# Products of the first four units written to idle tiles, and the second and third input sets loaded earlier

## The chip, the cores and the metric

The kernel runs on one core of a Trainium2 chip. The metric is the time of one execution on the device in microseconds; the median of several runs is given. Where the text speaks of a profiled execution, it is one execution that the hardware profiler recorded.

## The reference

```python
def _attn_ref(r, k, v, w, a, b):            # all (4, 8, 768, 40)
    state = zeros(B, H, D, D)
    for t in range(S):
        y[:, :, t] = einsum('bhd,bhde->bhe', r[t], state)
        Sa = einsum('bhde,bhe->bhd', state, a[t])
        state = state * w[t][..., None, :] - einsum('bhd,bhe->bhde', Sa, b[t])
        state = state + einsum('bhd,bhe->bhde', v[t], k[t])

def reference(**kwargs):
    x = _attn_ref(...)                       # -> (4, 768, 320)
    u = x + ((x^T @ U) @ V)^T
    x = u + relu(u @ w_ch1) @ w_ch2
    return four softmax-attention experts on x, top 2 of 4 by a gate, mixed
```

Only the first stage, the recurrence, is touched. All of it is float32.

## The kernel before

The recurrence is computed in chunks of 64 steps. There are 12 chunks and two pairs of batches, so 24 units; a unit is eight pairs of heads wide. Instead of stepping through time, a unit forms 64x64 products of its inputs (TensorE), inverts triangular blocks (VectorE) and passes a state to the next chunk.

The inputs w, a, b, k come packed in 16 sets (ld) of 128 rows, 1028.5 KB each. A set m has rows 0:40 and 64:104 for a unit of its own, and in the rows between a half of a third unit, a guest: sets 0 and 1 hold units 0 and 1 and the halves of unit 2, sets 2 and 3 units 3, 4 and the halves of 5. `slot(j)` (L95) gives set j its place: sets 0 and 1 two tiles ldt, sets 2 and 3 a part of the tiles xs that is written much later, sets 4 and 5 ldt again.

The steps around the change, each a generator whose next part one letter of a hand-written string ORDER_R (L44) runs:

- m, `loads` (L177): DMAs of the sets on SP's queue. Set 0 is loaded before the string begins (L464 to 467) and so is the first part of set 1; sets 1 to 3 come in three parts, the later ones whole.
- d, `scaled(j)` (L183), all on VectorE: a scan of w into P (L195), a reciprocal and a reverse scan (L200, L203), the scaled b and k into bkt (L208), the scaled a (F, L216), and two DMAs of F into the unit's tile ga (L219).
- g, `sent(j)` (L166): DMAs of the guest's rows from P, bkt and F to the guest's tiles P_g, bkt_g and ga (L164). P and bkt have two buffers each, P_g and bkt_g one.
- f, `front(u)` (L223), in five parts: transposes of P (pt) with their eviction (L233, L235); transposes of bkt in two halves (pb, L243, L244); the products of bkt and ga in two halves (pg, L255), which ACT evicts over bkt itself (L258). After the second half POOL copies four 32x256 blocks into lx (L263), masks two blocks into ga (L266) and copies two into m21 (L270).
- l, `more`/`tick`: one VectorE step of `lanes(g)` (L275), which inverts the 32x32 blocks of four units together. It starts with a transpose of lx (L279), so it needs the lx copies of all four units of its group.
- z, `ready` (L445), POOL memsets of uv, xu, sbd with st, and rbd; y, `firsts` (L451), the first loads of v (uv) and r (rbd, uvt, rpt).

Every engine runs its instructions in the order in which the string brings them (manual_schedule, L471); only semaphores make one engine wait for another. SP's queue issues all of the DMAs here and waits in order too. `later`/`passed` (L141, L154) put off some VectorE work by a count of steps of the string; a step added to the string lowers these counts as well.

In the string the products of units 0, 1, 2 and 3 end at positions 38, 51, 65 and 90; the memsets of sbd and st come at 88, the one of rbd at 105, the first loads into rbd and uvt at 106.

Of the kernel before, what the change touches and what calls it, by code (L numbers as in the profile page):

```python
# [11 lines left out]
F32 = mybir.dt.float32  # L12
# [3 lines left out]
AF = mybir.ActivationFunctionType  # L16
# [25 lines left out]

WAIT = (2, 3, 3)
ORDER_R = (  # L44
    'zddlllllldllllmgdlmgdlzfdldlglfmfgfzdgfdmfllyfgmlfffmfdfdfmmddllfflglmlgdffddgdglgllffldzl',
    'ffglldllllmlllfzylflllldflllflylfffldllflgldflflglffldlggylllfllgdmBffllAfflflflfffgAldlll',
    'BlmdlllfdfBgABAfqBAllfqlqBAddlgllldgmpdpldBlgllAqpgllfBAlffBAqfqqfpBAppflgllldddllffBmlffl',
    'qplfllqfqldpdlglflAlqffflBAgqplBdAgBlAfpqBpAplmlldldlfgdllgpqqBllllAflfglplAlBpfplAlBllAfl',
    'llfqBpfAmBqgqpdAlflldqlldlllllflffplqqgBlddfflllpplglfmlAdBggfdqllfpBABAflpllqBllplqlfddll',
    'glflqlfdfplBlfflmdpgqABfpfqlqldfABpABpplAllgfAqgBldqmAlfpdfdlplglffgBgllfplfddlfqllpffAfdl',  # L50
    'lgfqlqlAfllflllmlllBlAfABppABpgqfBqlqAddppfgllAllBlqdqllpdfggBlqlqldffAlBgAlBfpAqlpqBlffll',
    'ffflfllpflflfllpulpqAlBplAqlqBAllulqBllAlpqBpAxBlqlllxlllAlppqllxxlBAlllqulpBAqlqlBlABplpl',
    'AllppBxqllllqlllllAqlllpBplqqlABullplqBAllBAlpqplquBAllpqlpxxllluBApqpBlAqqlBAlluBAlqqppAq',
    'qpxlllullxxqppqllpqulplqlBplllxxllx',
)


def recurrence(ctx, tc, ld, vin, rv, ident, xs, keep, wpool, mix):
# [40 lines left out]
    BK, GA, PC, LX, M21, TF, UP = {}, {}, {}, {}, {}, {}, {}

    def load_ld(j, a=0, b=LDW):
        nc.sync.dma_start(slot(j)[:, a:b], ld[j, :, a:b])
# [63 lines left out]
    def sent(j):  # L166

        m, r = divmod(j, 2)
        f3 = slot(j)[:, :3 * PP * C].rearrange("p (k q t) -> p k q t", k=3, t=C)
        away(guests[0], PF[3 * m + r], r)  # L170
        yield
        away(guests[1], BKT[3 * m + r], r)
        yield
        away(GA[3 * m + 2][:, r], f3[:, 2], r)
        yield

    def loads():  # L177
        for j in range(1, NSET):
            for y in parts[j == 1:] if j < 4 else ((0, LDW),):
                load_ld(j, *y)  # L180
                yield

    def scaled(j):  # L183

# [38 lines left out]
    def front(u):  # L223

        g, uu = divmod(u, GU)
        c, bp = divmod(u, NBP)
        P, early = PF[u], u < GU
        pc = PC[u] = const.tile([128, PP], F32, tag="pc", bufs=16, name=f"pc{u}")
        nc.scalar.activation(pc, P[:, :, C], AF.Copy)
        pt = ps.tile([128, 4, 2, D], F32, tag="f", bufs=3, name=f"pt{u}")  # L230
        for p in range(4):
            for b in range(2):
                nc.tensor.matmul(pt[64 * b:64 * b + 64, p], P[:, 2 * p + b, :C],  # L233
                                 ident.rearrange("p (r e) -> p r e", r=2)[:, :, :D], start=True, stop=True)
# [815 lines left out]
```

## Time and profile before

| | us |
|---|---|
| median of 3 runs (lowest, highest) | 854.38 (853.5, 856.28) |
| the profiled execution, whole | 858.54 |
| its span, first to last instruction | 856.8 |

| engine | busy in the span, us | share |
|---|---|---|
| PE (TensorE) | 780.3 | 91% |
| PE's weight loads | 666.2 | 78% |
| DVE (VectorE) | 579.5 | 68% |
| ACT (ScalarE) | 469.9 | 55% |
| POOL (GpSimd) | 323.9 | 38% |

The recurrence takes about the first 325 us. There DVE is busy in nearly every slice of the page but the first two, and PE works at a share that rises from 0.5 to nearly 1; after that PE alone is nearly always busy.

How to read it: times are microseconds from the start of the span, unless marked ns. L258 is line 258 of the kernel. In a timeline a row has start, duration, engine, line, operation, tile written <- tile read, the shape and the count of what was merged; in brackets the idle time of that engine before it and what ended that. In a list of waits a row has who waited for whom, the sum in us, the number of times and the longest. SPq is the queue of SyncE, whose durations are those of issuing a DMA, not of the transfer. PEclk is the granted TensorE clock, 1.00 for 2.4 GHz and 0.50 for 1.2 GHz.

### The profile page before, as it was taken

Reading aid. Unit: us, or ns where it says so; the run is one execution under the profiler, and the core shown is the slowest. Engines: PE = TensorE matmul, PEld = TensorE weight load, DVE = VectorE, ACT = ScalarE, POOL = GpSimd, SP = SyncE. Lnnn points to the kernel's source line nnn. Section 1 sums busy time; section 2 is a strip of 40 time slices with the busy share of each in tenths; the row PEclk is TensorE's granted clock in tenths of the full one; section 3 lists DMA queues with packets and bytes.
Section 4 is the critical chain, followed back from the end, with each engine's and each line's share of the span. In section 5 each row is a group of like instructions: output and inputs, shape, how many; then the busy total and the mean of one; then the engine's idle time right before and its main releaser. Section 6 shows DMA issues by size and latency. Waiting matters only on the chain.

```text
span 856.8 us, 22703 instructions
## 1 busy us (share of the span) xinstructions
PE 780.3 (91%) x9100; PEld 666.2 (78%) x9100; DVE 579.5 (68%) x1388; ACT 469.9 (55%) x1125; POOL 323.9 (38%) x456
## 2 busy tenths in 40 slices
PE   5666989989999897989899999999999999999997
PEld 4555888988898687877678888887778788887875
DVE  6599999988998997448624131322268868778773
ACT  3534867766677678723323231312168757767672
POOL 5664464536545324315513220202027344244430
PEclk9787999998999999899999999999999999999999
DMA  5554256555545364512100100000000010000101
GB/s 166 171 143 158 78 171 164 151 144 150 137 144 145 87 171 114 130 54 83 47 1 25 34 2 1 1 1 0 1 1 2 1 47 2 16 32 2 47 2 47
DMA packets 53201, 61.47 MB, mean 72 GB/s; under 512 B 31208, under 2 KB 38376, under 8 KB 51560
## 3 DMA queue, kind: packets, MB, share of 16 engines
q1 hardware_dynamic: 53096, 60.02, 24.6%
q8 instruction: 72, 1.18, 0.6%
q14 instruction: 33, 0.27, 0.1%
HBM read 47.46 MB, written 4.13 MB: 60 GB/s over the span
## 4 chain that ended last, share of the span: by engine, by line
PE 54%; DVE 19%; DMA 6%; issue 5%; ACT 4%; POOL 2%; SPq 1%; DVEq 0%; POOLq 0%; ACTq 0%
PE po L943 4%; PE ph L743 3%; PE pa L760 3%; PE ph L740 3%; PE pa L761 3%; PE pa L762 3%; PE ph L741 3%; PE ph L739 3%; PE tp L930 3%; DVE lt L288 3%; DVE tmp L285 3%; PE pn L403 2%; PE pw L343 2%; PE ps L890 2%; PE ps L889 2%
## 5 line engine op out<-in xcount | busy, mean ns | idle before, releaser
L913 POOL TENSOR_TENSOR P<-P,sm 128x128 f32<-128x128 f32 (+2 forms) x92 | 82.9, 931 | 127.6 <-DVE sm L903 115.4
L747 DVE SCALAR_TENSOR_TENSOR hl<-ph,hh 128x512 fp32r<-128x512 f32 x60 | 41.1, 690 | 118.6 <-ACT hh L746 116.1
L746 ACT ACTIVATE hh<-ph 128x512 fp32r<-128x512 f32 x60 | 35.1, 594 | 108.5 <-PE pa L762 101.2
L894 ACT ACTIVATE P<-ps,mx 128x640 f32<-128x640 f32 (+4 forms) x96 | 60.5, 634 | 26.1 <-DVE mx L892 18.1
L285 DVE TENSOR_TENSOR tmp<-lt 128x30 f32<-128x30 f32 (+9 forms) x180 | 70.3, 390 | 3.9
L288 DVE TENSOR_TENSOR lt<-lt,tmp 128x30 f32<-128x30 f32 (+9 forms) x180 | 69.0, 384 | 3.7
L892 DVE CUSTOM_DVE_ANT_0 ps<-ps,neg 128x640 f32<-128x640 f32 (+4 forms) x96 | 59.0, 639 | 7.6 <-PE ps L890 6.5
L263 POOL COPY lx<-bkt 32x256 f32<-32x256 f32 x64 | 30.0, 469 | 87.9 <-ACT bkt L258 85.8
L403 PE MATMUL pn<-rbd,uvt 128*128 128x128 f32 x384 | 54.9, 293 | 7.3 <-DMA uvt<-in_rin 5.7
L776 POOL TENSOR_TENSOR t<-t,ul 128x512 f32<-128x512 f32 x12 | 15.4, 1294 | 116.8 <-DVE t L775 116.7
L255 PE MATMUL pg<-ga,bkt 128*128 128x128 f32 x256 | 40.1, 318 | 19.6 <-DMA ga<-ldt 14.3
L403 PEld LDWEIGHTS pn<-rbd,uvt 128*128 128x128 f32 x384 | 49.6, 204 | 9.5 <-issue 4.9
L930 PE MATMUL tp<-ident,P 128*128 128x128 f32 x336 | 52.0, 276 | 1.8 <-ACT pt L934 0.8
L255 PEld LDWEIGHTS pg<-ga,bkt 128*128 128x128 f32 x256 | 36.6, 226 | 21.6 <-issue 12.7
L346 ACT ACTIVATE uv<-pw 32x320 f32<-32x320 f32 x96 | 41.1, 428 | 18.4 <-PE pw L343 16.7
L739 PE MATMUL ph<-uh,w 128*128 128x512 f32 x120 | 47.1, 399 | 1.7 <-ACT uh L728 1.6
L740 PE MATMUL ph<-ul,w 128*128 128x512 f32 x120 | 47.7, 397 | 0.6 <-DVE ul L729 0.6
L741 PE MATMUL ph<-uh,w 128*128 128x512 f32 x120 | 47.3, 396 | 0.0
L761 PE MATMUL pa<-hl,w 128*128 128x512 f32 x120 | 47.1, 392 | 0.0
L930 PEld LDWEIGHTS tp<-ident,P 128*128 128x128 f32 x336 | 39.4, 140 | 9.2 <-POOL P L913 2.7
L943 PE MATMUL po<-pt,vals 128*64 128x256 f32 (+3 forms) x320 | 45.1, 397 | 1.4 <-DVE o L959 1.0
L762 PE MATMUL pa<-hh,w 128*128 128x512 f32 x120 | 46.2, 391 | 0.0
(217 smaller groups left out, 2239.8 us busy)
## 6 DMA issues: line engine op xcount, KB each, us to landing
ldt<-in_ld SPq DMA_DIRECT2D x12, 1028.5 KB
uvt<-in_rin SPq DMA_DIRECT2D x48, 128.0 KB
rpt<-in_rin SPq DMA_DIRECT2D x24, 256.0 KB
rbd<-in_rin SPq DMA_DIRECT2D x48, 96.0 KB
uv<-in_vin SPq DMA_DIRECT2D x48, 80.0 KB
out<-o SPq DMA_DIRECT2D x24, 160.0 KB
ga<-ldt SPq DMA_DIRECT2D x28, 80.0 KB
room<-in_w SPq DMA_DIRECT2D x7, 320.0 KB
```

The source lines that it names most:

```text
L255: nc.tensor.matmul(pg[:, p], bkt[:, h * HP + p].rearrange("p k t -> p (k t)"), ga[:, :, h * HP + p], start=True, stop=True)
L285: nc.vector.tensor_tensor(tv, L[:, s + 1:, s:s + 1].to_broadcast([128, n, s]), L[:, s:s + 1, :s].to_broadcast([128, n, s]), op=OP.mult)
L288: nc.vector.tensor_tensor(L[:, s + 1:, :s], L[:, s + 1:, :s], tv, op=OP.add)
L403: nc.tensor.matmul(pn[h][:, p], ut[:, h * HP + p].rearrange("p r t -> p (r t)"), rbd[u % 2][:, :, h * HP + p], start=True, stop=True)
L739: nc.tensor.matmul(ph, w[:, 0, f], uh[:, ft], start=ft == 0, stop=False)
L740: nc.tensor.matmul(ph, w[:, 0, f], ul[:, ft], start=False, stop=False)
L741: nc.tensor.matmul(ph, w[:, 1, f], uh[:, ft], start=False, stop=False)
L761: nc.tensor.matmul(pa[ft], w[:, o:o + m], hl, start=False, stop=False)
L762: nc.tensor.matmul(pa[ft], w[:, 2 * DM - FT[2][0] + o:2 * DM - FT[2][0] + o + m], hh, start=False, stop=last)
L913: nc.gpsimd.tensor_tensor(p, p, sm[:, i:i + 1].to_broadcast([128, w]), op=OP.mult)
L930: nc.tensor.transpose(pt[:, j - j0], P[:, c:c + 128], ident)
L943: nc.tensor.matmul(po[64 * r:64 * r + 64, s0:w], VS[b][:, j, HD * e:HD * e + HD], PT[r][:, j, s0:], start=j == 0, stop=j == i1 - 1, skip_g ...
```

## The change

Three edits, all in `recurrence`.

1. The products of units 0 to 3 (`early`) are evicted not over bkt but to four tiles that are idle at that time, viewed in bkt's shape: rbd0, rbd1, uvt0 and uvt1 (`rooms`). POOL reads them from there (gm).
2. POOL's two masks into ga and two copies into m21 become a generator of their own, `kept(u)`, with a letter k. In the string each k stands right behind the f that ends its unit's products. Beside k's that are added and m's that are taken out, the order of all other steps is the same, also with the works that are put off.
3. Sets 0 and 1 are loaded on SP ahead of the string, in three parts each. Set 2 is loaded in two parts on ACT's queue at the string's start. Sets 3 and later are loaded whole, set 3 by the first m left in the string; it stands behind unit 1's products and ahead of the DMAs of F for unit 3.

```diff
-    def load_ld(j, a=0, b=LDW):
-        nc.sync.dma_start(slot(j)[:, a:b], ld[j, :, a:b])
+    rooms = [t.rearrange("p r q t -> p (r q t)").rearrange("p (q r t) -> p q r t", q=PP, r=2) for t in rbd] + uvt
+    def load_ld(j, a=0, b=LDW, queue=nc.sync):
+        queue.dma_start(slot(j)[:, a:b], ld[j, :, a:b])
...
     def loads():
-        for j in range(1, NSET):
-            for y in parts[j == 1:] if j < 4 else ((0, LDW),):
-                load_ld(j, *y)
-                yield
+        for j in range(3, NSET):
+            load_ld(j)
+            yield
...
-            nc.scalar.activation(bkt[:, hs], pg, AF.Copy)
+            gm = GM[u] = rooms[u] if early else bkt
+            nc.scalar.activation(gm[:, hs], pg, AF.Copy)
...
-                        nc.gpsimd.tensor_copy(LX[g][q, uu * PP:uu * PP + PP], bkt[q, :, r, 32 * i:32 * i + 32])
-                for r in range(2):
-                    ... affine_select(ga[z, r], bkt[z, :, r], ...)
-                for r in range(2):
-                    ... tensor_copy(m21[q], bkt[q, :, r, 32:])
+                        nc.gpsimd.tensor_copy(LX[g][q, uu * PP:uu * PP + PP], gm[q, :, r, 32 * i:32 * i + 32])
...
+    def kept(u):
+        ga, gm = GA[u], GM[u]
+        m21 = M21[u] = const.tile([128, PP, 32], F32, tag="m21", bufs=AHEAD + 1, name=f"m21{u}")
+        for r in range(2):
+            ... affine_select(ga[z, r], gm[z, :, r], ...)
+        for r in range(2):
+            ... tensor_copy(m21[q], gm[q, :, r, 32:])
+        yield
...
-    for a, b in parts:
-        load_ld(0, a, b)
-    load_ld(1, *parts[0])
+    for j in range(2):
+        for a, b in parts:
+            load_ld(j, a, b)
...
+    for a, b in (parts[0], (0, n)):
+        load_ld(2, a, b, nc.scalar)
...
+            "k": chain(*[kept(u) for u in range(NU)]), ...
```

The first two lines of the string, before and after:

```diff
-    'zddlllllldllllmgdlmgdlzfdldlglfmfgfzdgfdmfllyfgmlfffmfdfdfmmddllfflglmlgdffddgdglgllffldzl',
-    'ffglldllllmlllfzylflllldflllflylfffldllflgldflflglffldlggylllfllgdmBffllAfflflflfffgAldlll',
+    'zddlllllldllllgdlgdlzfdldlglffgfzdgfkdfllyfglfffkmfdfdfddllffklglmlgdffddgdglgllffldzlfkfg',
+    'lldllllmlllfzylflllldflllfklylfffldllflgldfklflglffldlggylllfllgdmBfkfllAfflflfklfffgAldll',
```

## Rows read from the trace of the kernel before

**Rows 1.** Busy time by stretch, 42 to 100 us.

```profile
core 0: us, PE busy (x) PEld busy (x) DVE busy (x) ACT busy (x) POOL busy (x), PEclk, DMA share, GB/s
...
42.00:60.00 18.00, 13.04 (x140) 11.73 (x141) 17.02 (x35) 6.45 (x15) 11.45 (x22) 0.84 0.58 151
60.00:80.00 20.00, 9.74 (x155) 8.84 (x152) 18.62 (x46) 7.04 (x18) 8.88 (x15) 0.74 0.55 174
80.00:100.00 20.00, 18.04 (x465) 16.24 (x464) 19.48 (x41) 16.51 (x38) 10.29 (x16) 1.00 0.18 49
```

**Rows 2.** Timeline of DVE, 0 to 45 us.

```profile
13.79 0.69 DVE L216 SCALAR_TENSOR_TENSOR ldt<-ldt,P 128x512 f32<-128x512 f32 x1 [0.79 <-DMA ldt<-in_ld]
...
17.24 1.31 DVE L195 TENSOR_TENSOR_SCAN P<-x,hot 128x520 f32<-128x520 f32 x1 [2.73 <-PE pt L233]
...
18.82 1.45 DVE L203 TENSOR_TENSOR_SCAN x<-x,hot 128x520 f32<-128x520 f32 x1
24.31 1.45 DVE L208 TENSOR_TENSOR bkt<-x 128x1024 f32<-128x1024 f32 x1 [4.04 <-DMA x<-in_ld]
...
30.84 1.32 DVE L208 TENSOR_TENSOR bkt<-x 128x1024 f32<-128x1024 f32 x1 [0.20 <-ACT pc L229]
32.08 0.88 DVE L216 SCALAR_TENSOR_TENSOR x<-x,P 128x512 f32<-128x512 f32 x1
...
36.05 1.24 DVE L195 TENSOR_TENSOR_SCAN P<-ldt,hot 128x520 f32<-128x520 f32 x1 [3.07 <-DMA ldt<-in_ld]
...
41.57 1.97 DVE L279 STREAM_TRANSPOSE lt<-lx 128x1024 f32<-128x1024 f32 x1 [2.76 <-POOL lx L263]
```

**Rows 3.** Timeline of POOL, 0 to 50 us.

```profile
16.64 2.55 POOL L263 COPY lx<-bkt 32x256 f32<-32x256 f32 x4 [9.17 <-ACT bkt L258]
19.26 2.17 POOL L266 TENSOR_SCALAR_AFFINE_SELECT ga<-bkt 64x512 f32<-64x512 f32 x2
...
24.03 2.24 POOL L266 TENSOR_SCALAR_AFFINE_SELECT ga<-bkt 64x512 f32<-64x512 f32 x2
...
30.69 2.97 POOL L263 COPY lx<-bkt_g 32x256 f32<-32x256 f32 x4 [3.62 <-ACT bkt_g L258]
33.73 1.35 POOL L266 TENSOR_SCALAR_AFFINE_SELECT ga<-bkt_g 64x512 f32<-64x512 f32 x2
35.04 0.84 POOL L270 COPY m<-bkt_g 32x256 f32<-32x256 f32 x2
35.93 1.20 POOL L448 MEMSET sbd<- 128x640 f32 x2
37.08 0.66 POOL L448 MEMSET st<- 128x320 f32 x2
39.84 1.69 POOL L263 COPY lx<-bkt 32x256 f32<-32x256 f32 x4 [2.11 <-ACT bkt L258]
```

**Rows 4.** Timeline of ACT, 0 to 45 us.

```profile
23.39 1.99 ACT L129 ACTIVATE ga<-zero 128x1024 f32<-128x1024 f32 x2
...
38.70 1.09 ACT L258 ACTIVATE bkt<-pg 128x512 f32<-128x512 f32 x2 [5.31 <-DMA bkt_g<-bkt]
```

**Rows 5.** Waits of SP's queue, 0 to 60 us: sum, times, longest.

```profile
SPq L164 <- POOL m L270: 4.4, 1, 4.4
```

**Rows 6.** Timeline of SP's queue, 0 to 50 us.

```profile
0.82 2.28 SPq L102 DMA_DIRECT2D ldt<-in_ld  x5
...
16.05 1.51 SPq L219 DMA_DIRECT2D ga<-ldt  x2
...
30.80 0.58 SPq L102 DMA_DIRECT2D ldt<-in_ld  x1
```

**Rows 7.** DMA rate in 40 equal slices of 0 to 60 us.

```profile
GB/s 0 106 374 359 407 40 20 105 257 66 201 87 120 137 323 134 294 191 332 100 89 121 406 187 68 96 93 72 104 77 99 335 386 231 144 107 112 56 115 55
DMA packets 5190, 9.90 MB, mean 165 GB/s; under 512 B 1912, under 2 KB 2168, under 8 KB 4928
```

**Rows 8.** Timeline of PE, 0 to 45 us.

```profile
12.16 3.78 PE L255 MATMUL pg<-ga,bkt 128*128 128x128 f32 x16 [1.81 <-DMA ga<-ldt]
...
19.27 2.02 PE L255 MATMUL pg<-ga,bkt 128*128 128x128 f32 x16 [1.05 <-DMA ga<-ldt]
...
26.74 3.25 PE L255 MATMUL pg<-ga,bkt_g 128*128 128x128 f32 x16 [3.72 <-DMA ga<-ldt]
```

More of the change, by code (lines that the diff above doesn't have):

```diff
@@ L44 @@
 ORDER_R = (
-    'zddlllllldllllmgdlmgdlzfdldlglfmfgfzdgfdmfllyfgmlfffmfdfdfmmddllfflglmlgdffddgdglgllffldzl',
-    'ffglldllllmlllfzylflllldflllflylfffldllflgldflflglffldlggylllfllgdmBffllAfflflflfffgAldlll',
[L47 to L54, printed above, removed]
+    'zddlllllldllllgdlgdlzfdldlglffgfzdgfkdfllyfglfffkmfdfdfddllffklglmlgdffddgdglgllffldzlfkfg',
+    'lldllllmlllfzylflllldflllfklylfffldllflgldfklflglffldlggylllfllgdmBfkfllAfflflfklfffgAldll',
+    'lBlmdlllfdfkBgABAfqBAllfqlqBAddlgllldgmpdpldBlgllAqpgllfBAlffkBAqfqqfpBAppflgllldddllffkBm',
+    'lfflqplfllqfqldpdlglfklAlqffflBAgqplBdAgBlAfpqBpAplmlldldlfkgdllgpqqBllllAflfglplAlBpfplAl',
+    'BllAflllfkqBpfAmBqgqpdAlflldqlldlllllflffkplqqgBlddfflllpplglfmlAdBggfdqllfkpBABAflpllqBll',
+    'plqlfddllglflqlfdfkplBlfflmdpgqABfpfqlqldfkABpABpplAllgfAqgBldqmAlfpdfdlplglffkgBgllfplfdd',
+    'lfqllpffkAfdllgfqlqlAfllflllmlllBlAfkABppABpgqfBqlqAddppfgllAllBlqdqllpdfggBlqlqldffkAlBgA',
+    'lBfpAqlpqBlffllffkflfllpflflfkllpulpqAlBplAqlqBAllulqBllAlpqBpAxBlqlllxlllAlppqllxxlBAlllq',
+    'ulpBAqlqlBlABplplAllppBxqllllqlllllAqlllpBplqqlABullplqBAllBAlpqplquBAllpqlpxxllluBApqpBlA',
+    'qqlBAlluBAlqqppAqqpxlllullxxqppqllpqulplqlBplllxxllx',
 )
@@ L98, in recurrence @@
     mix.spare = lambda: fpool.tile([128, 2 * (S // 4)], F32, tag="lx", name="spare")
[L99 to L102 removed]
+    BK, GA, GM, PC, LX, M21, TF, UP = {}, {}, {}, {}, {}, {}, {}, {}
+    def load_ld(j, a=0, b=LDW, queue=nc.sync):
+        queue.dma_start(slot(j)[:, a:b], ld[j, :, a:b])
     def load_v(u):
@@ L248, in front @@
         ga = GA[u]
-        m21 = M21[u] = const.tile([128, PP, 32], F32, tag="m21", bufs=AHEAD + 1, name=f"m21{u}")
         if uu == 0:
@@ L262, in front @@
                         q = slice(64 * r + 32 * i, 64 * r + 32 * i + 32)
-                        nc.gpsimd.tensor_copy(LX[g][q, uu * PP:uu * PP + PP], bkt[q, :, r, 32 * i:32 * i + 32])
-                for r in range(2):
-                    z = slice(64 - 64 * r, 128 - 64 * r)
-                    nc.gpsimd.affine_select(ga[z, r], bkt[z, :, r], [[0, PP], [1, C]], OP.is_gt, 0.0, base=0,
-                                            channel_multiplier=-1)
-                for r in range(2):
-                    q = slice(64 * r, 64 * r + 32)
-                    nc.gpsimd.tensor_copy(m21[q], bkt[q, :, r, 32:])
+                        nc.gpsimd.tensor_copy(LX[g][q, uu * PP:uu * PP + PP], gm[q, :, r, 32 * i:32 * i + 32])
             if h and uu == GU - 1:
@@ L273, in front @@
             yield
+    def kept(u):
+        ga, gm = GA[u], GM[u]
+        m21 = M21[u] = const.tile([128, PP, 32], F32, tag="m21", bufs=AHEAD + 1, name=f"m21{u}")
+        for r in range(2):
+            z = slice(64 - 64 * r, 128 - 64 * r)
+            nc.gpsimd.affine_select(ga[z, r], gm[z, :, r], [[0, PP], [1, C]], OP.is_gt, 0.0, base=0,
+                                    channel_multiplier=-1)
+        for r in range(2):
+            q = slice(64 * r, 64 * r + 32)
+            nc.gpsimd.tensor_copy(m21[q], gm[q, :, r, 32:])
+        yield
     def lanes(g):
@@ L475, in recurrence @@
             "d": chain(*[scaled(j) for j in range(NSET)]),
-            "g": chain(*[sent(j) for j in range(NSET)]), "m": loads(), "y": firsts(), "f": fronts(), "z": ready(), "l": more(),
+            "g": chain(*[sent(j) for j in range(NSET)]), "m": loads(), "y": firsts(), "f": fronts(),
+            "k": chain(*[kept(u) for u in range(NU)]), "z": ready(), "l": more(),
             "u": mix.weights(mix.sources()[0], ldt, (guests[0].rearrange("p q t -> p (q t)"), hot)),
```

## The prediction

> **What bounds the kernel now.** I read the views in this order: busy time by stretch, then the timeline of each engine in the first 45 us with what ended its pauses, then the DMA's rate there. Busy time by stretch [rows 1] shows VectorE (DVE) as the engine without slack from 42 us on: 17.0 of 18 us, 18.6 of 20, 19.5 of 20, while TensorE (PE) is at 13.0 and 9.7 of the first two stretches. Its pauses there add up to 2.9 us between 122 instructions, so none is a wait worth the name. The last one that is ends at 41.57 us: 2.76 us, for POOL's copies into lx (L263), and with it the first group's `lanes` starts, by its transpose (L279) [rows 2]. So everything after 41.57 us runs on one engine's clock, started by the fourth unit's lx copies. A change ahead of that point is worth what it moves 41.57 to, and no more.
>
> What made the copies late: POOL began them at 39.84, after an eviction (L258) that ACT started at 38.70 after 5.31 us of waiting for the DMA bkt_g<-bkt [rows 3, 4]. The eviction overwrites bkt in place, so it must wait until unit 5's guest rows have been sent out of it. That DMA in turn stood on SP for 4.4 us behind POOL's m21 copies (L270) [rows 5], which still read bkt_g of unit 2. This circle is what the change opens.
>
> **The change part by part.** Times are the profiled execution's: span 856.8 us, whole time 858.54, that is 4.16 above the median 854.38. I work out a difference and take it off the median.
>
> *Evictions to idle tiles* (units 0 to 3, eight ACTIVATEs): same count, same 128x512 shape (1.09 us for two [rows 4]), no new instruction. Removed: the wait for bkt_g<-bkt ahead of those of units 0, 1 and 3, and the hold that POOL's readers had on bkt and bkt_g. The rooms are rbd and uvt; rbd's memset and the first loads into both stand behind `kept(3)` in program order anyway, so nothing new waits for them.
>
> *`kept` as a step of its own*: each k stands right behind the fifth f of its unit, so POOL's order is what it was: lx, affine selects (L266), m21, unit by unit, then sbd and st, then unit 3's lx. Taking loads and k's out, the whole later order is unchanged, also the delayed DVE works. Cost and gain 0.
>
> *Loads*: SP issued five ahead in 2.28 us [rows 6], so a sixth costs 0.46 us in time in which SP is idle. Two for set 2 go to ACT, which has nothing else to do until DVE's first scan has made P; at about 0.6 us each (one load's issue is 0.58 [rows 6]) I cost them at nothing, and at 1.2 us on ACT if that cover were gone. They put 3.09 MB up front instead of 1.8 MB. The slices of 1.5 us in 3 to 7.5 us moved 374, 359 and 407 GB/s [rows 7]; begun at some 2.6 us, three sets and P_g are through by 2.6 + 3.17 MB / 385 GB/s = 10.8 us, ahead of unit 0's ga rows, which land at 12.16, where PE's first product starts [rows 8]. So I leave unit 0's products and the first lx copies at 16.64 where they are [rows 3], and keep a delay of up to 1.5 us for the range.
>
> Gone from SP are the loads that stood between the guests' DMAs. Unit 1's ga rows (16.05 us, 1.51 of issue, product at 19.27, so landed 1.7 us after issue [rows 6, 8]) go out at 14.7 and land at 17.9; the product takes 2.0 us and the eviction is done by 20.8. Unit 2's ga rows are issued by 20.25 and land at 22.0 instead of 26.74, where PE had waited 3.72 us for them [rows 8]; the eviction, behind ACT's two blank tiles (1.99 us [rows 4]), is done at 25.6. Set 3, now whole, is issued at 20.3 to 20.9. Set 4 took from 31.38 to 36.05, 4.7 us, to land [rows 2, 6], so set 3 lands at 25.6. Unit 3's ga rows wait on SP for their blank tile (23.5) and are there by 26.8, its product is evicted by 29.9. Set 4 goes out at 26.4 to 27.0 and lands at 31.7.
>
> DVE then runs set 2's steps in 13.8 to 18.6 (set 1's F no longer waits 0.79 us for its load [rows 2], and set 2 is there), set 3's from 25.6, set 4's two scans from 31.7, and is free for `lanes` at 34.4. If nothing else were late, `lanes` would start there, 7.1 us earlier.
>
> *What is late next: POOL.* From 16.64 on it never waits, as each eviction (20.8, 25.6, 29.9) is there before it comes to it. Its bare sum up to unit 3's lx, by rows without a long DVE operation beside them [rows 3]: lx 1.69, affine selects 1.35, m21 0.84, thrice: 11.64; sbd and st 1.20 + 0.66 = 1.86; the last lx 1.69; with 0.3 for the gaps 15.5. That ends at 32.1 us.
>
> But POOL and DVE hold each other up. With a scan at 17.24 beside it lx took 2.55 (0.86 over), the selects with a scan at 18.82 took 2.17 (0.82 over), with the product into bkt at 24.31 2.24 (0.89 over), and lx with two such operations, at 30.84 and 32.08, took 2.97 (1.28 over) [rows 2, 3]. Five DVE operations cost POOL 3.85 us, 0.77 each. The memsets beside the scan at 36.05 took nothing more. Before, sets 3 and 4 mostly met an idle POOL or its memsets; now POOL has no pause, so eight such operations fall on its copies and selects: set 2's bkt and F, set 3's two scans, bkt and F, set 4's two scans. 8 x 0.77 = 6.2 us, and lx ends at 38.3. The bounds: no hold at all, then DVE's 34.4 decides; each of the eight for its whole length (six of 1.24, two of 0.69 [rows 2], 8.8 us), 40.9. I take 0.77 since it comes from the same tiles and engines.
>
> The Trainium skill (SBUF — State Buffer, on the ports that DVE and GpSimd share) says that the pair is an exclusive lock, and that a DVE operation with two SBUF inputs and a GpSimd one that reads SBUF fully block each other. By that rule the whole lengths would count, and `lanes` would start at 40.9 us, 0.7 us earlier than now; the measured 0.77 is less, and the sum goes by it.
>
> So `lanes` starts at 38.3 us instead of 41.57: 3.2 us earlier. From there to 100 us DVE has no pause to lose it in [rows 1], the later order is the old one, and set 5 and unit 4's ga rows, which follow on SP, come some 6 us earlier, so they don't take over. Forecast: 854.38 - 3.2 = 851.2, with 34.4 to 40.9 as the far ends of `lanes`, 847.2 to 853.7.
>
> **The rivals.**
> (1) *The hold is cheap.* Sets 3 and 4 meet POOL's memsets or its waits, and POOL ends at 33 to 36: 5.5 to 7.1 us earlier, at 6.4 us 848.0. For it: the memsets are free, and a later set 4 would meet them. Against it: four of four rows in which POOL and a long DVE operation overlap show the price.
> (2) *Nothing left.* Each of the eight operations holds POOL for its whole length (40.9), or 1 to 2 us of delay at unit 0's ga rows on top of the forecast, leaves 0 to 1.5 us: 853.6. For it: each eats most of 3.2 us. Against: the measured price and the rate in the first slices.
> (3) *The preloads crowd out unit 0, and it gets slower.* Set 1 is now ahead of unit 0's ga rows on SP's queue and set 2 beside it on ACT's. PE's first product waits for them. At the page's rate of the mixed stretches, say 165 GB/s (the mean of 0 to 60 us [rows 7]), 3.17 MB last until 21.8 us, the rows land 11 us later, and since set 2's operations are then past when POOL begins, `lanes` starts at 28 + 15.5 + 4.6 = 48: 6.6 us later, 861. It decides from about 250 GB/s down: there the rows land 4.8 us later, which takes back the 3.2 us and the 1.5 us of set 2's holds that fall away. Against: 359 to 407 GB/s in just this traffic.
>
> **How the numbers follow.** Forecast (2 to 4.4 us earlier, 850.0 to 852.4) 0.58; rival 1 0.18; rival 2 0.18; rival 3 0.06. A measurement of this kernel tells about 0.3%, 2.6 us, from no change, so faster means below 851.8: rival 1 and about 0.65 of the forecast, 0.18 + 0.38 = 0.56. Slower is rival 3, 0.05 of it beyond 0.3%. The same is the rest, 0.39. The range must leave out at most 0.2: from 847.8 (rival 1's most likely half is in) to 853.8 (most of rival 2 is in).
>
> **What would show it.** In the trace after: no wait of ACT's first eight L258 for bkt_g<-bkt; POOL's idle time between 16.6 us and unit 3's lx near 0, and lx and selects of units 2 and 3 longer than 1.69 and 1.35; DVE waiting 3 to 4 us at L279 for POOL's lx; L279 at 38.3 (37 to 39.6). The forecast is wrong if L279 stands before 36.5 (the hold is cheap) or after 40.5; wrong in its first step if the first L255 starts after 13 us instead of at 12.16; and wrong in its last if L279 moves and the end doesn't move with it, which a wait of DVE between there and 100 us would show.

## The result and the profile after

| | before | after |
|---|---|---|
| median (lowest, highest) of 20 runs each, taken together, us | 856.96 (853.5, 865.03) | 851.68 (844.78, 863.1) |
| ratio of the two, with its 95% interval | | 0.992 [0.9899, 0.9942] |
| profiled execution, whole, us | 858.54 | 846.52 |
| its span, us | 856.8 | 844.8 |

The changed kernel is faster by 0.8%, more than the 0.3% that the prediction calls measurable. The forecast was 851.2 within 847.8 to 853.8, so the median fell into the range. The forecast difference was 3.2 us; by medians it is 5.3, and over all the runs below 4.8 ± 1.1 (± is a 95% interval throughout). That the median comes within 0.5 us of the forecast is luck: the forecast was taken off a median of three runs, 854.38, which 20 runs put at 856.96, so a base 2.6 us too low made up for a gain about 2 us too small. The mechanism has to be looked at apart from the size. Where means or ratios are given, runs more than 1.5% above the fastest of the same kernel measured together are left out (2 of 44 of the changed kernel, 5 of the 105 of before that have a clock on record); with them the difference is the same 4.8 us.

Lines have moved: the products are L254 now (were L255), the copies into lx L263 as before, the masks L274 (L266), the copies into m21 L278 (L270), the transpose of `lanes` L285 (L279), its steps L291 and L294.

Timeline of POOL after, from 17 to 42 us (start, duration, operation; in brackets the idle time before it):

```profile
17.21 3.08 POOL L263 COPY lx<-rbd 32x256 f32<-32x256 f32 x4 [9.74 <-ACT rbd L258]
...
22.53 1.70 POOL L263 COPY lx<-rbd 32x256 f32<-32x256 f32 x4
...
26.52 2.74 POOL L263 COPY lx<-uvt 32x256 f32<-32x256 f32 x4
29.33 3.06 POOL L274 TENSOR_SCALAR_AFFINE_SELECT ga<-uvt 64x512 f32<-64x512 f32 x2
32.34 2.23 POOL L278 COPY m<-uvt 32x256 f32<-32x256 f32 x2
34.63 1.20 POOL L454 MEMSET sbd<- 128x640 f32 x2
35.78 0.66 POOL L454 MEMSET st<- 128x320 f32 x2
36.50 1.69 POOL L263 COPY lx<-uvt 32x256 f32<-32x256 f32 x4
```

Timeline of DVE after, 5 to 41 us:

```profile
5.08 1.24 DVE L195 TENSOR_TENSOR_SCAN P<-ldt,hot 128x520 f32<-128x520 f32 x1 [1.42 <-DMA ldt<-in_ld]
...
17.56 1.23 DVE L208 TENSOR_TENSOR bkt<-x 128x1024 f32<-128x1024 f32 x1
18.70 0.89 DVE L216 SCALAR_TENSOR_TENSOR x<-x,P 128x512 f32<-128x512 f32 x1
...
27.39 1.24 DVE L195 TENSOR_TENSOR_SCAN P<-x,hot 128x520 f32<-128x520 f32 x1 [7.77 <-DMA x<-in_ld]
...
28.90 1.45 DVE L203 TENSOR_TENSOR_SCAN x<-x,hot 128x520 f32<-128x520 f32 x1
30.44 1.43 DVE L208 TENSOR_TENSOR bkt<-x 128x1024 f32<-128x1024 f32 x1
31.80 1.13 DVE L216 SCALAR_TENSOR_TENSOR x<-x,P 128x512 f32<-128x512 f32 x1
...
33.14 1.24 DVE L195 TENSOR_TENSOR_SCAN P<-ldt,hot 128x520 f32<-128x520 f32 x1 [0.19 <-ACT bk L244]
...
34.66 1.24 DVE L203 TENSOR_TENSOR_SCAN ldt<-ldt,hot 128x520 f32<-128x520 f32 x1
38.23 1.95 DVE L285 STREAM_TRANSPOSE lt<-lx 128x1024 f32<-128x1024 f32 x1 [2.33 <-POOL lx L263]
```

What is to be seen: POOL, which in [rows 3] paused for 3.62 and 2.11 us ahead of units 2 and 3, has no pause left from 17.21 us to the copies of unit 3. The rows that are longer than their bare 1.69, 1.35 and 0.84 are those beside DVE's operations on sets 2, 3 and 4; the copies of unit 1, with DVE idle beside them, took 1.70. The transpose of `lanes` starts at 38.23 us instead of 41.57 [rows 2], and what it waits for is still POOL's lx.

Timeline of PE after, the products of units 0 and 2:

```profile
13.10 3.41 PE L254 MATMUL pg<-ga,bkt 128*128 128x128 f32 x16 [1.99 <-DMA ga<-ldt]
...
23.70 2.02 PE L254 MATMUL pg<-ga,bkt_g 128*128 128x128 f32 x16 [0.98 <-DMA ga<-ldt]
```

Against [rows 8], unit 2's product stands at 23.70 instead of 26.74 and unit 0's at 13.10 instead of 12.16. The waits of ACT after, 0 to 60 us (sum, times, longest), hold no wait of the evictions into rbd and uvt for a DMA; the 5.31 us of [rows 4] are gone:

```profile
ACT rbd L258 <- PE pg L254: 6.1, 4, 3.6
...
ACT uvt L258 <- PE pg L254: 1.1, 3, 0.6
```

Busy time by stretch after, with the columns of [rows 1]; DVE is as full as before:

```profile
60.00:80.00 20.00, 13.07 (x236) 11.99 (x238) 18.62 (x47) 7.39 (x17) 9.02 (x17) 0.74 0.53 168
80.00:100.00 20.00, 18.13 (x448) 16.36 (x448) 19.48 (x42) 16.15 (x38) 9.35 (x15) 1.00 0.16 41
```

The starts of the transposes of the six groups follow a shift through the recurrence. Those of before, of a second profiled execution of before (below), and of three of the changed kernel, in us:

| group | 1 | 2 | 3 | 4 | 5 | 6 | whole |
|---|---|---|---|---|---|---|---|
| before | 41.57 | 79.34 | 128.26 | 181.16 | 233.81 | 279.72 | 858.54 |
| before, second | 41.32 | 79.00 | 127.61 | 182.89 | 235.75 | 281.16 | 856.71 |
| after | 38.23 | 75.85 | 124.85 | 177.47 | 227.21 | 273.03 | 846.52 |
| after, second | 37.87 | 75.56 | 124.23 | 182.18 | 234.00 | 280.06 | 854.45 |
| after, third | 38.23 | 75.88 | 124.75 | 178.21 | 228.58 | 274.78 | 850.89 |

Up to the third group the changed kernel is 3.3 to 3.5 us ahead of the first execution of before, in each of its first and third executions, and 3.7 to 4.0 in its second. Behind that the executions of the changed kernel part by 4.7 to 7 us, although their starts lie within 0.4 us of each other; the experiments look for the reason in PE's clock.

### The profile page after: what moved, and what is told of

The parts are those of the page before. It is cut to its first block, busy times and chain, and to the rows that moved or that the text cites. A ratio compares the mean times of both kernels' runs of the same rounds, so it can differ in the third digit from the quotient of the medians.

```text
span 844.8 us, 22681 instructions
## 1 busy us (share of the span) xinstructions
PE 772.3 (91%) x9100; PEld 658.6 (78%) x9100; DVE 576.9 (68%) x1388; ACT 471.5 (56%) x1125; POOL 328.8 (39%) x456
## 3 DMA queue, kind: packets, MB, share of 16 engines
q10 hardware_dynamic: 288, 1.05, 0.3%
## 4 chain that ended last, share of the span: by engine, by line
PE 56%; DVE 18%; issue 6%; ACT 5%; DMA 5%; POOL 2%; SPq 2%; DVEq 0%; ACTq 0%; POOLq 0%
PE po L952 4%; PE tp L939 3%; PE ph L752 3%; PE pa L769 3%; PE pa L770 3%; PE pa L771 3%; PE ph L749 3%; PE ph L750 3%; PE ph L748 3%; DVE lt L294 3%; DVE tmp L291 3%; PE pn L409 2%; PE ps L899 2%; PE ps L898 2%; PE pg L254 2%
## 5 line engine op out<-in xcount | busy, mean ns | idle before, releaser
L291 DVE TENSOR_TENSOR tmp<-lt 128x30 f32<-128x30 f32 (+9 forms) x180 | 69.4, 385 | 3.9
L294 DVE TENSOR_TENSOR lt<-lt,tmp 128x30 f32<-128x30 f32 (+9 forms) x180 | 69.4, 385 | 3.8
L409 PE MATMUL pn<-rbd,uvt 128*128 128x128 f32 x384 | 51.4, 280 | 9.1 <-DMA rpt<-in_rin 3.6
L254 PE MATMUL pg<-ga,bkt 128*128 128x128 f32 x256 | 39.6, 315 | 20.5 <-DMA ga<-ldt 16.0
L263 POOL COPY lx<-bkt 32x256 f32<-32x256 f32 x52 | 25.6, 493 | 77.2 <-ACT bkt L258 70.8
L409 PEld LDWEIGHTS pn<-rbd,uvt 128*128 128x128 f32 x384 | 45.9, 191 | 12.0 <-issue 4.7
L254 PEld LDWEIGHTS pg<-ga,bkt 128*128 128x128 f32 x256 | 36.1, 224 | 22.8 <-issue 14.0
```

Of the source, the lines that this page charges most:

```text
L291: nc.vector.tensor_tensor(tv, L[:, s + 1:, s:s + 1].to_broadcast([128, n, s]), L[:, s:s + 1, :s].to_broadcast([128, n, s]), op=OP.mult)
L294: nc.vector.tensor_tensor(L[:, s + 1:, :s], L[:, s + 1:, :s], tv, op=OP.add)
L409: nc.tensor.matmul(pn[h][:, p], ut[:, h * HP + p].rearrange("p r t -> p (r t)"), rbd[u % 2][:, :, h * HP + p], start=True, stop=True)
```

## The experiments

The theory is that of the prediction: the start of the first `lanes` is what counts, POOL's sum with its holds by DVE sets it, and the whole kernel moves by as much. The rivals were that only one of the two edits matters, that the holds are not what makes POOL late, that something else sets the end (a shift of the start isn't carried there), or that more than the shift arrives.

| run | group 1 starts | group 2 starts | median (runs), us | ratio to before [95%] |
|---|---|---|---|---|
| e1, changed kernel again | 37.87 | 75.56 | 852.62 (12) | 0.9961 [0.9934, 0.9988] |
| e2, delayed | 42.48 | 80.22 | 856.45 (12) | 1.0009 [0.998, 1.0038] |
| e3, masks late | 36.72 | 77.27 | 853.45 (12) | 0.9962 [0.993, 0.9995] |
| e4, rooms only | 40.57 | 78.29 | 852.75 (12) | 0.9956 [0.9925, 0.9986] |
| e5, loads only | 41.70 | 79.43 | 856.4 (12) | 0.9996 [0.9962, 1.0029] |
| e6, early zero | 37.01 | 74.64 | 850.4 (12) | 0.9928 [0.9898, 0.9959] |
| e7, and m21 by ACT | 36.48 | 74.02 | 848.64 (9) | 0.9899 [0.9868, 0.993] |
| e8, and loads ahead | 38.80 | 76.93 | 854.68 (12) | 0.9971 [0.9938, 1.0004] |
| e9, before again | 41.32 | 79.00 | 855.67 (12) | 0.9984 [0.9952, 1.0015] |
| e10, changed kernel, third | 38.23 | 75.88 | 851.98 (12) | 0.9942 [0.9907, 0.9977] |
| e11, e7 again | 36.24 | 73.64 | 847.28 (10) | 0.9905 [0.9873, 0.9937] |
| e12, far delayed | 55.13 | 92.78 | 867.1 (6) | 1.0129 [1.0083, 1.0174] |

**Each edit alone.** e4 is the kernel before with the idle tiles as the target of the evictions and nothing else. e5 is the changed kernel with the evictions back in bkt:

```diff
-            gm = GM[u] = rooms[u] if early else bkt
+            gm = GM[u] = bkt
```

> The kernel before with the evictions to idle tiles alone, all loads as before. Unit 3's eviction no longer waits for bkt_g<-bkt; it comes when its product is done (33.9 us) and POOL is through with unit 2 and the memsets (37.7), so lx is done at 39.4: lanes at 39.5, 2.1 us earlier than before, ratio near 0.9975. If the loads were needed for it, lanes stays at 41 or later and the time stays.

> The changed kernel with its products evicted over bkt again: the new loads alone. Unit 3's eviction waits once more for bkt_g<-bkt, and that for POOL's m21 copies of unit 2, which end near 34.5; the DMA is issued by 35.9, lands at 37.6, the eviction is done at 38.7 and lx at 40.5: lanes at 40.5, 1.1 us earlier than before, ratio 0.9985. If the rooms bring nothing and the loads all, lanes is at 38.2 as in the changed kernel and the ratio near 0.995.

Rooms alone start `lanes` at 40.57, some 0.9 us earlier than the two executions of before; loads alone at 41.70, not earlier at all. Both together give 3.3 us of start. What stops each alone stands in its POOL timeline, of e4 first and of e5 second:

```profile
30.73 3.07 POOL L265 COPY lx<-uvt 32x256 f32<-32x256 f32 x4 [2.98 <-ACT uvt L260]
...
37.94 2.60 POOL L265 COPY lx<-uvt 32x256 f32<-32x256 f32 x4
```

```profile
27.09 4.60 POOL L263 COPY lx<-bkt_g 32x256 f32<-32x256 f32 x4
...
39.98 1.69 POOL L263 COPY lx<-bkt 32x256 f32<-32x256 f32 x4 [2.10 <-ACT bkt L258]
```

With rooms alone unit 2's copies into lx come as late as before (30.73, [rows 3] has 30.69): a set's load is still issued ahead of its ga rows on SP, at 19.09 us, and the rows land 3.9 us after their issue, in the changed kernel 1.5. With loads alone unit 2 is early (27.09), but the circle through bkt_g is closed, and ACT stands for it. Timeline of ACT in e5:

```profile
38.83 1.09 ACT L258 ACTIVATE bkt<-pg 128x512 f32<-128x512 f32 x2 [10.40 <-DMA bkt_g<-bkt]
```

For the start of `lanes` the two edits are worth something only as a pair: the loads bring unit 2 forward, the rooms unit 3. The expectations had 39.5 for e4 and 40.5 for e5; both came about 1 us later, e4 since unit 3's copies met one more scan (2.60 instead of 1.69), e5 since POOL's m21 copies of unit 2, for which the eviction waits by way of the DMA, ended at 36.0 and not near 34.5. For the time it is not shown of both: loads alone are 4.5 ± 2.2 us slower than the changed kernel, but rooms alone only 1.1 ± 1.7, though they start `lanes` 2.3 us later. The time of e4 moved by 3.7 ± 1.6 us against before, more than its start (0.9); the surplus that all the kernels tried here show against before is a part of it, and the rest stays open (below).

**The start moved back.** e2 delays POOL in the changed kernel by ten more memsets of st ahead of unit 3's copies, e12 by forty:

```diff
-        for x in (uv[:2], uv[2:], xu, sbd + st, rbd):
+        for x in (uv[:2], uv[2:], xu, sbd + st + st[:1] * 10, rbd):
```

> The changed kernel with ten more memsets of st (0.33 us each, 3.3 us) on POOL ahead of unit 3's lx copies, so that lanes starts at 41.5 us as before, with the new loads and rooms in place. If the start of lanes is all that the change is worth (A and B alike), its time is that of the kernel before, ratio 0.998 to 1.002. If the loads' new places or fewer transfers beside the later work bring something of their own, it stays 2 to 4 us faster, ratio 0.995 to 0.998.

> The changed kernel with forty memsets of st (0.41 us each, 16.5 us) on POOL ahead of unit 3's lx copies: lanes at 54.8 us, 13.2 us later than before. By A the time is 13.2 us longer, 870, ratio 1.0155; if a microsecond at the start of lanes is worth 1.3 at the end, as a line through the runs so far has it, 17 us longer, ratio 1.020.

The group of memsets took 4.78 us in e2 and 17.45 in e12 (0.66 without the addition). `lanes` started at 42.48 (1 us past the 41.5 expected, since a memset of st took 0.41 us in such a row and not 0.33) and at 55.13, the second group at 80.22 and 92.78, and the times went to 1.0009 and 1.0129 of before. POOL timeline and transpose of e12:

```profile
35.89 17.45 POOL L454 MEMSET st<- 128x320 f32 x42
53.41 1.69 POOL L263 COPY lx<-uvt 32x256 f32<-32x256 f32 x4
```

```profile
55.13 1.92 DVE L285 STREAM_TRANSPOSE lt<-lx 128x1024 f32<-128x1024 f32 x1 [19.35 <-POOL lx L263]
```

So with both edits in place, a late start of `lanes` alone takes the gain away: it doesn't come from the evictions, the loads or the split of the step by themselves. The right measure is the changed kernel itself, from which both differ by the delay alone: the second group comes 4.5 us later in e2 and 17.0 in e12, and the time is 4.9 ± 1.6 and 15.5 ± 2.4 us longer. So the shift arrives one to one. Against the runs of before, e12's 13.6 us of shift raised the time by 10.6 ± 2.3 us, less than the shift. Of the two ratios expected, 1.0155 lies within the interval and 1.020 doesn't: no surplus grows with the shift.

**What makes POOL late.** e3 lets POOL copy lx for all four units first, and the masks and copies of units 0 to 2 follow unit 3's lx:

```diff
-    'zddlllllldllllgdlgdlzfdldlglffgfzdgfkdfllyfglfffkmfdfdfddllffklglmlgdffddgdglgllffldzlfkfg',
+    'zddlllllldllllgdlgdlzfdldlglffgfzdgfdfllyfglfffmfdfdfddllfflglmlgdffddgdglgllffldzlfkkkkfg',
```

> The changed kernel with the steps k of units 0 to 2 moved behind unit 3's lx copies, so that POOL's masks and m21 copies (6.6 us bare, with what scans add to them) no longer stand ahead of lanes. If POOL's sum and its meetings with DVE are what is late, lanes starts when DVE is done with set 4's scans, at 35.9 to 36.5 us instead of 38.2, and the time falls by 2 us more (ratio to before lower by 0.0025). If another wait stood right behind POOL, lanes stays at 37.5 or later and the time stays.

POOL's copies were done at 33.45, and DVE came to the transpose without a wait, at 36.72. But the second group started at 77.27, only 1.9 us earlier than before; the changed kernel has 75.8. Timeline of DVE in e3, the first steps of `lanes`:

```profile
38.67 0.20 DVE L291 TENSOR_TENSOR tmp<-lt 128x30 f32<-128x30 f32 x1
...
40.12 1.00 DVE L294 TENSOR_TENSOR lt<-lt,tmp 128x30 f32<-128x30 f32 x1
41.16 0.68 DVE L291 TENSOR_TENSOR tmp<-lt 128x58 f32<-128x58 f32 x1
```

In the changed kernel the L294 at this place took 0.20:

```profile
41.49 0.20 DVE L294 TENSOR_TENSOR lt<-lt,tmp 128x30 f32<-128x30 f32 x1
```

and the next L291 0.22. The holds work in both directions: POOL's work that is put behind the start of `lanes` takes time from DVE, which has no slack. Set 4's F comes 10.05 us after the transpose instead of 8.65, and the second group 40.55 instead of 37.62; the 1.5 us of this that are lost further on were not followed up. By the start of the second group the order of the change, masks first, is the better one; by time the two are not told apart (e3 1.7 ± 2.2 us longer).

e6 takes the memsets of sbd and st off the stretch, by a z moved forward in the string to where POOL is idle. e7 also gives the m21 copies of units 0 to 3 to ACT, behind unit 3's copies:

```diff
-    'zddlllllldllllgdlgdlzfdldlglffgfzdgfkdfllyfglfffkmfdfdfddllffklglmlgdffddgdglgllffldzlfkfg',
+    'zddlllllldllllgdlgdlzfdldlglffgfzzdgfkdfllyfglfffkmfdfdfddllffklglmlgdffddgdglgllffldlfkfg',
...
-        for r in range(2):
-            q = slice(64 * r, 64 * r + 32)
-            nc.gpsimd.tensor_copy(m21[q], gm[q, :, r, 32:])
+        for v in range(GU) if u == GU - 1 else [u] if u >= GU else []:
+            for r in range(2):
+                q = slice(64 * r, 64 * r + 32)
+                copy = nc.gpsimd.tensor_copy if v >= GU else lambda y, x: nc.scalar.activation(y, x, AF.Copy)
+                copy(M21[v][q], GM[v][q, :, r, 32:])
```

> The changed kernel with the memsets of sbd and st (1.86 us on POOL) moved from ahead of unit 3's lx to behind those of xu, where POOL has nothing to do. No read of SBUF by POOL is moved. If POOL's sum is what is late, lanes starts 1.5 to 1.9 us earlier, at 36.0 to 36.5 us, which is also where DVE is done with set 4's scans, and unlike with the masks moved the second group's transpose keeps it (74.0 instead of 75.8). If something else is, lanes stays at 38.

> As the kernel with the early memsets, and the m21 copies of units 0 to 3 (0.82 us each unit) done by ACT behind unit 3's eviction. POOL's sum is 2.5 us shorter, ending near 34; then DVE's own scans of set 4 (done at 35.9, its load landing at 33.1) are late, so lanes starts at 36.0, no more than 0.4 us ahead of the kernel with the early memsets. If POOL were still the later one, lanes would follow it below 36.

> The kernel with the early memsets and ACT's m21 copies a second time: lanes at 36.5 us, 1.6 us ahead of the changed kernel. By A 5.1 us faster than before, ratio 0.994; by B, and by its first ratio, 0.990.

POOL in e6:

```profile
34.42 2.55 POOL L263 COPY lx<-uvt 32x256 f32<-32x256 f32 x4
```

The memsets are worth 1.86 us of POOL, and `lanes` moved by 1.2 (38.23 to 37.01, against 36.0 to 36.5 expected). Most of what is missing went back to the hold: the scan that had met the memsets (34.66 beside 34.63 above) meets unit 3's copies now, 2.55 instead of 1.69. With the m21 copies gone as well, `lanes` starts at 36.48 and 36.24 with no wait for POOL. DVE in e7:

```profile
27.19 1.24 DVE L195 TENSOR_TENSOR_SCAN P<-x,hot 128x520 f32<-128x520 f32 x1 [7.44 <-DMA x<-in_ld]
...
34.82 1.74 DVE L203 TENSOR_TENSOR_SCAN ldt<-ldt,hot 128x520 f32<-128x520 f32 x1
36.48 1.94 DVE L287 STREAM_TRANSPOSE lt<-lx 128x1024 f32<-128x1024 f32 x1
```

Now DVE is late itself: it waited for set 3's load until 27.19, and POOL's copies beside set 4's two scans hold them (1.44 and 1.74 instead of 1.24). This version ran at 848.64 and 847.28, 0.9899 and 0.9905 of before, and is 3.7 ± 1.4 us faster than the changed kernel, so it beats both.

**Loads still further ahead.** e8 is e7 with set 3 on ACT's queue behind the second of unit 0's evictions of bk, and set 4 on SP where set 3 stood; for that one m of the string comes earlier:

```diff
-            load_ld(j)
+            load_ld(j, queue=nc.scalar if j == 3 else nc.sync)
...
-    'zddlllllldllllgdlgdlzfdldlglffgfzzdgfkdfllyfglfffkmfdfdfddllffklglmlgdffddgdglgllffldlfkfg',
+    'zddlllllldllllgdlgdlzfdldlglffmgfzzdgfkdfllyfglfffkmfdfdfddllffklgllgdffddgdglgllffldlfkfg',
```

> As the one with ACT's m21 copies, and set 3 loaded on ACT's queue behind unit 0's second bk eviction (11 us), set 4 on SP where set 3 stood. DVE then runs set 3's steps at 19.6 to 25, set 4's scans from 29 to 31.7, and POOL's sum (bare 11.1 us without memsets and m21, 6.2 of holds, from 17.2) ends at 34.5: lanes at 34.5, 3.7 us earlier than in the changed kernel, and the time 7 us below before, ratio 0.992. If the fourth set crowds the guests' DMAs, the first lx copies start after 18.5 us and lanes is at 36 or later.

It was to make DVE early. Instead unit 0's products became late. The queues of SP and ACT in e8, then PE and DVE, and the DMA rate in slices of 1.5 us from 0:

```profile
9.86 1.55 SPq L219 DMA_DIRECT2D ga<-ldt  x2
```

```profile
10.89 0.34 ACTq L103 DMA_DIRECT2D x<-in_ld  x1
```

```profile
17.54 3.75 PE L254 MATMUL pg<-ga,bkt 128*128 128x128 f32 x16 [6.69 <-DMA P_g<-P]
```

```profile
38.80 1.99 DVE L287 STREAM_TRANSPOSE lt<-lx 128x1024 f32<-128x1024 f32 x1 [3.32 <-POOL lx L263]
```

```profile
GB/s 0 140 333 335 423 364 408 263 176 324 294 132 90 122 114 69 269 389 44 52 91 88 96 90 59 111 78 180 395 317 194 118 0 0 107 112 56 111 63 99
```

The first product starts at 17.54, 4.4 us after that of the changed kernel, though its ga rows were issued at the same time (9.86 here, 9.85 there) and ahead of set 3's load. (The profile puts the wait down to the P_g DMA, which stands behind them on SP's queue.) Meanwhile the rate stands at 324 and 294 GB/s in the slices from 13.5 to 16.5 us, where the changed kernel had 75 and 57. This is what rival 3 of the prediction feared, with one more load of 1 MB. Where between three and four sets the edge lies was not tried.

**The same kernel again, and what the clock does.** e1 and e10 are the changed kernel, e9 is the kernel before.

> The changed kernel once more, beside the kernel before on the same chip. Its first profile had lanes start 3.3 us earlier than before, the recurrence's last tf transpose 7.3 us and the end 12 us earlier, with 27 us of the granted clock at its lower level against 51 us. Theory A (the shift is all, what comes on top is the clock's chance): lanes at 38.2 again, about 3.3 us faster than before at equal granted clock, ratio near 0.996, and the gain beyond 3.3 us comes and goes with the falls of the clock. Theory B (the earlier start also takes away something later): ratio again near 0.992, 6 to 7 us.

> The changed kernel a third time, since 0.992 and 0.9961 differ by more than the 3.4 us in question. Theory A (the end moves as lanes does): lanes at 37.9 to 38.3 us, ratio near 0.996. Theory B (something later gives as much again): ratio near 0.992.

> The kernel before, profiled a second time. Its first profile had the granted clock at the lower level at 208 to 215 us, which no profile of the other kernels has at that place. If that fall was chance, the second profile has it elsewhere or not at all, and the recurrence's later transposes come 2 to 3 us earlier than in the first with the start of lanes unchanged at 41.6 us; the ratio is 1.000 within 0.003. If the fall belongs to the old order, it is at 208 to 215 us again.

The start of `lanes` repeats within 0.4 us. The end doesn't, and the ratios don't decide between the two theories: e1 came out as A (0.9961), e11 as B (0.9905), e10 between (0.9942). Before's fall of the clock is at 211 to 218 us again in e9. Busy time by stretch in the second execution of the changed kernel (e1), and below it the same stretches of the first:

```profile
115.00:120.00 5.00, 2.58 (x59) 2.29 (x59) 4.61 (x17) 1.89 (x6) 4.68 (x9) 0.82 0.56 223
120.00:125.00 5.00, 5.00 (x86) 4.50 (x84) 4.96 (x6) 1.74 (x4) 4.65 (x8) 0.50 0.09 32
125.00:130.00 5.00, 5.00 (x78) 4.61 (x76) 3.25 (x9) 1.28 (x3) 1.45 (x3) 0.50 0.39 88
130.00:135.00 5.00, 5.00 (x114) 4.91 (x109) 1.87 (x6) 3.58 (x9) 0.00 (x0) 0.50 0.50 125
```

```profile
115.00:120.00 5.00, 3.61 (x70) 3.33 (x70) 4.64 (x14) 2.87 (x8) 4.74 (x8) 1.00 0.85 295
120.00:125.00 5.00, 4.53 (x128) 4.10 (x125) 4.93 (x11) 2.98 (x7) 4.59 (x8) 1.00 0.08 27
125.00:130.00 5.00, 4.98 (x150) 4.64 (x149) 4.90 (x11) 3.07 (x8) 2.06 (x4) 1.00 0.44 101
130.00:135.00 5.00, 5.00 (x132) 4.78 (x132) 4.80 (x16) 3.64 (x10) 0.00 (x0) 1.00 0.50 126
```

In e1 PE was granted 1.2 GHz from about 118 to 138 us, behind a stretch in which it was busy for 2.58 of 5 us. It then did 86 and 78 matmuls in 5 us instead of 128 and 150, and DVE, which otherwise has no pause there, came down to 1.87 of 5 us. The fourth group started 4.7 us later than in the first execution, the same kernel. One such fall costs as much as the change gains.

The other place is 208 to 218 us. Both profiled executions of before have a fall to 0.50 there, behind a wait of PE of 1.48 us for DVE's uvt (L396). Before's second execution (e9), and the third of the changed kernel (e10), same stretch:

```profile
207.50:210.00 2.50, 1.02 (x32) 0.86 (x29) 2.47 (x6) 1.81 (x5) 2.33 (x5) 1.00 0.41 116
210.00:212.50 2.50, 2.50 (x66) 2.19 (x64) 2.40 (x8) 0.67 (x3) 0.19 (x1) 0.67 0.23 53
212.50:215.00 2.50, 2.50 (x58) 2.41 (x58) 1.64 (x3) 1.71 (x4) 0.00 (x0) 0.50 0.85 219
```

```profile
210.00:212.50 2.50, 2.50 (x25) 2.50 (x24) 2.50 (x8) 2.39 (x8) 0.27 (x1) 1.00 0.11 25
```

None of the other twelve profiled executions (the three of the changed kernel and those of the experiments) has a fall between 200 and 220 us. Four of them (e1, e7, e10, e12) have one of about 3.4 us further on, just ahead of the fifth group's transpose (222 to 226 us in e10); in before's two it is 6.8 us long. From group 3 to group 5 the lead over before's first execution grows from 3.4 to 6.6 us in the first of the changed kernel and from 3.5 to 5.2 us in the third.

**Does more than the shift arrive?** The mean times of the runs that are kept, against the mean of before's 100 with a clock on record (856.63 us), beside the shift of the second group (before: 79.17, the mean of two):

| kernel (runs) | group 2 moved by | time moved by | beyond the shift |
|---|---|---|---|
| changed kernel (42) | -3.4 | -4.8 ± 1.1 | -1.4 |
| e2 (12) | +1.1 | 0.0 ± 1.5 | -1.0 |
| e3 (12) | -1.9 | -3.2 ± 2.1 | -1.3 |
| e4 (12) | -0.9 | -3.7 ± 1.6 | -2.8 |
| e5 (11) | +0.3 | -0.3 ± 2.1 | -0.6 |
| e6 (12) | -4.5 | -5.6 ± 2.0 | -1.1 |
| e7 and e11 (19) | -5.3 | -8.5 ± 1.2 | -3.2 |
| e8 (12) | -2.2 | -2.4 ± 2.1 | -0.2 |
| e12 (6) | +13.6 | +10.6 ± 2.3 | -3.0 |

The last column has no clear trend with the shift, from -5.3 to +13.6. But all nine lie below zero, by 1.6 us in the mean. A time of before goes with the run's mean granted clock (correlation -0.82, 0.47 us less for 0.001 more over its 100 runs), and the changed kernel's 42 runs have a mean clock of 0.9731 against 0.9684. Compared at the same clock it is faster by 2.6 ± 0.7 us; the other 2.2 go with the higher clock. In the same way e3, e6 and e7 with e11 gain 2.0, 4.2 and 5.2 us, beside shifts of 1.9, 4.5 and 5.3. But e4 (rooms alone) gains 2.5 ± 1.1 beside 0.9, e8 0.2 ± 1.2 beside 2.2, and e12 loses 8.4 ± 1.6 beside 13.6. The mean clock also moves with the start itself (0.9637 in e12, 0.9753 in e7 and e11), so comparing at the same clock can take away a part of the shift. That the surplus is one of clock is therefore likely, and not shown. Whether it comes from the fall at 208 to 218 us, which both profiled executions of before have and no other has, stays open: were it in every run of before and in none of the others, the last column would be -3 throughout, which e7 with e11, e4 and e12 have, and the other six don't.

## Why the prediction was right, and where it was off

**What bounds the kernel: right.** The fourth unit's copies into lx release DVE, and what DVE does from there on follows their start: 18.62 of 20 us busy in 60 to 80 us and 19.48 in 80 to 100, to the digit the numbers of [rows 1]. From the first group's start to the second's it is 37.4 to 37.8 us in every execution but those of e3 (40.55) and e8 (38.13), wherever the first begins. e2 and e12 moved that start alone and the time went with it.

**The circle through bkt_g: right, and needed with the loads.** ACT's evictions of units 0 to 3 wait only for PE. e5 closes the circle again and the gain is gone. That the loads alone give nothing and the rooms alone next to nothing of the start was in the prediction only by its sums, not said; what the rooms alone gave in time (e4) none of its terms explains.

**Unit 0 stays where it is: wrong by 0.9 us.** The first product starts at 13.10, past the 13 us that the prediction set for it. The prediction counted only when all three sets would be through (10.8 us), and let unit 0's own set come as it had before. In the trace ACT's queue issues set 2 at once, beside SP's first loads:

```profile
0.82 0.41 ACTq L103 DMA_DIRECT2D x<-in_ld  x1
...
1.55 0.33 ACTq L103 DMA_DIRECT2D x<-in_ld  x1
```

So set 2's transfer runs beside set 0's from the start, and DVE's first scan began at 5.08 us (4.31 in the trace of before). The Trainium skill (DMA: Bandwidth & Descriptors, section Queues, rings and completion order) says that a DMA engine takes turns between the queues that have work; the 0.77 us agree with that. In the other executions with these loads the scan came at 4.59 to 4.89 us, and the product still at 12.98 to 13.25, apart from e8. No run has set 2 on ACT's queue without the rest of set 1 ahead on SP, so the share of each is not shown. 0.57 us reached POOL's first copies, at 17.21 instead of 16.64; in e1 and e10 it was 1.0 us. It lay inside the 1.5 us kept for the range.

**Sets 3 and 4: late by 1.4 to 1.8 us, without effect.** Set 3 was forecast to land at 25.6 and DVE took it at 27.39; its issue on SP was at 22.28 instead of 20.3, and it took 5.1 us instead of 4.7. Set 4's scan is at 33.14 instead of 31.7. DVE would have been free at 35.9, not 34.4, and so waited 2.33 us for POOL instead of 3.9. POOL was still later, so the sum didn't change.

**POOL is late next: right in place and sum, by terms that cancel.** POOL has no pause, and its bare sum is that of the prediction: 17.21 + 15.5 + the holds = 38.2. The holds are 1.39 (unit 0's lx), 1.05 (unit 2's lx), 1.71 (its masks) and 1.39 (its m21 copies), 5.5 us instead of 6.2. Seven operations and not eight paid: the eighth, the scan at 34.66, fell beside the memset of sbd, which took its bare 1.20, as [rows 3] had shown. Over seven that is 0.79 each, against 0.77. One hold too many and 0.57 us of start too early came out even: 38.23 against 38.3. That the sum hit to 0.1 us is luck; in e1 and e10 POOL starts at 17.63 and 17.64 and the holds come to 4.8 and 5.1 us. The section on the kernel says that only semaphores make one engine wait for another; these holds are waits without one. DVE pays as well, which the prediction left out: F of set 3 took 1.13 us instead of 0.69, its second scan 1.45 instead of 1.24.

The Trainium skill (SBUF — State Buffer, section Who interferes with whom) has the two engines block each other fully in such pairs. That each holds up the other the rows bear out, the hold on DVE in e3 included; the price here is 5.5 us for seven operations that by the prediction's bare 1.24 and 0.69 us last 7.6 together, less than their whole lengths. By the whole lengths `lanes` would have started at 40.3.

**The end moves by the same: right for the shift, short in the total.** That step failed in size: the prediction put at nothing whatever comes on top of the shift. The shift of 3.3 us is still there at 125 us, and by e2 and e12 against the changed kernel it arrives one to one. But the time moved by 4.8 ± 1.1. What is beyond the shift, 1.4 us in the mean, goes with the clock of PE as far as the runs tell, and its cause stays open; the prediction had looked at DVE's pauses only up to 100 us. The three executions of the changed kernel alone differ by 8 us with starts within 0.4.

**The rivals.** Rival 1 (the hold is cheap, 848.0) is out: `lanes` would start before 36.5, and it started at 38.23 with the holds as priced. It would have been the right time for e7, in which the copies under the hold are fewer. Rival 2 (nothing left) is out in the changed kernel by the same row, though unit 0's delay of about 1 us, one of its conditions, did come; fewer holds made up for it. Rival 3 (preloads crowd out unit 0) did not come here; e8 shows it, with one more load.

## What to carry to other kernels

Two waits that lie one behind the other on the way to the same instruction have to be removed together: of the start of `lanes`, each alone gave 0.9 us and none here, both 3.3. (In the time, rooms alone gave more than that, for a reason that stays open.) Before an engine is named as the next bound, its bare sum is to be taken from rows without a neighbour, and the neighbour's operations counted one by one against the rows that they will meet, since here a scan beside POOL's memsets cost nothing (1.20 us for the memset, as bare) and one beside its copies 0.86. Where an engine is full behind the point that moves, work postponed past that point can come back as a hold on it, as in e3.

## What the runs showed of the hardware that was not expected

- The run-to-run spread of one kernel here goes for the larger part with the granted clock (correlation -0.82). The changed kernel ran from 844.8 to 863.1 us; one stretch of 20 us at 1.2 GHz went with 5 us although DVE, not PE, had been the engine without slack. With 12 runs a difference was known to 1.5 to 2.1 us only.
- ACT's queue issues its first DMAs at 0.82 us, ahead of its first instruction (1.26), and so they run beside SP's first loads (DVE's first scan was 0.2 to 0.8 us later than before).
- Holds fall on both engines: a 0.20 us step of `lanes` took 1.0 us beside POOL's copies and masks in e3.
